# Four more copies of q by DMA, and one logarithm placed behind a copy: an attention kernel fused with a feed-forward network

## The chip, the cores and the metric

The kernel runs on one core of one Trainium2 chip. The metric is the device time in microseconds of one execution of the whole program. Three runs of the kernel before gave 288.22, 288.23 and 288.67 us; the median is 288.23 us.

## The reference

Eight batches of eight heads, 576 tokens, 64 numbers per head. Heads 0 to 3 ("plain") let a token see itself and the 31 tokens before it; heads 4 to 7 ("dilated") let it see every fourth token of the last 128. The result goes through a feed-forward network with a squared ReLU:

```python
scores = scale * np.matmul(q, k.transpose(0, 1, 3, 2))
scores = np.where(masks[None, :, :, :], scores, -1000000000.0)
attn = np.exp(scores - np.max(scores, axis=-1, keepdims=True))
attn = attn / (np.sum(attn, axis=-1, keepdims=True) + 1e-09)
x = np.matmul(attn, v)                       # then (tokens, 512)
h = np.maximum(x @ w_in, 0.0)                # w_in: 512 x 2048
out = h * h @ w_out                          # w_out: 2048 x 512
```

## The kernel before, in words

**The feed-forward network** works on nine tiles of 512 tokens. A tile is 32 *groups* of work. The first sixteen groups multiply by `w_in` (line 989): ScalarE takes each result out of its PSUM bank with a ReLU (line 1002), VectorE squares it (line 1005). The last sixteen groups multiply by `w_out`. From the fifth tile on this second half is done with seven products of half-size blocks, M1 to M7 (line 1152), of which some use sums of blocks that VectorE makes ahead (line 1046, "the sums"). In the fifth and the sixth tile the products run in this order on TensorE: M1, half of M2, M6, the other half of M2, M5, M7, M3, M4. M1, M6 and M5 share one PSUM bank, called X here: after M1 ScalarE copies the bank to SBUF (line 1066), after M6 a second time (line 1068), after M5 a third time (line 1068). M5 cannot start before the second copy has ended, because it overwrites the bank. M2's bank is added up by VectorE (line 1053).

**The attention** is not a stage of its own: its steps are hung between the groups of the network, so that TensorE goes from network to attention and back. All engines take their instructions in the order in which the program records them; nothing is reordered later. A list `steps` holds entries (group, rank, batch, code); it is sorted by group and rank, and after each group the entries that are due are recorded. In the fifth tile (groups 128 to 159, t = 128) the attention of batch 5 is finished, in the sixth tile (t = 160) that of batch 6. A pair of heads is called e (0 and 1 plain, 2 and 3 dilated). The codes that matter:

- `V`, a *visit* (function `quadrants`): TensorE computes scores of some pairs of heads and the products with v and with ones of others, in 64x64 quarters of the array (line 379). The visit at t+15 serves pairs 0 and 2 with products, the one at t+23 serves pairs 1 and 3 and computes the scores of the next batch's pairs 2 and 0.
- `E`: ScalarE's exponential of a score bank (line 745) and VectorE's mask (line 750).
- `L`: the logarithm of a pair's denominators on ScalarE, two instructions, 512 columns (line 712) and 64 columns (line 713). `X`: ScalarE's exponential of minus that logarithm (line 727), then VectorE's two products that write the normalised result to `xT` (lines 730 and 734).
- `K`, `R`, `Q` (function `arrange`): a batch's k, its end pieces and its plain q are put in the layout that the scores read. q and k come from HBM by GpSimd's queue (line 183) and are transposed by DMA from SP's queue into `qx` and `kx` (line 264). `Q` has eight copies for a batch, four of pair 0 and four of pair 1, in each case from one half of the partitions to one half.

The two places that the change touches, before it:

```python
# arrange, lines 342 to 347
if what == "Q" and (b == B - 1 or b == B - 2 and e == 1):
    nc.sync.dma_start(q_both[rows, hs, jj::2, :], qx[b % 2][src, hs, :, :])
elif what == "Q" and b == XB:
    ...
elif what == "Q":
    copy(q_both[rows, hs, jj::2, :], qx[b % 2][src, hs, :, :])

# the steps of a batch from the sixth on (quick), second half of its tile
visit(t + 15, [(b, 3), (b, 1)], [(b, 0), (b, 2)][: 1 + (b >= PAIRED)])
...
expo(3, *[t + 16 + quick] * 2)
norm(0, t + 17 + 2 * quick)          # L0 at t + 19, X0 at t + 20
visit(t + 23, [(b + 1, 2), (b + 1, 0)] if after else [], [(b, 1), (b, 3)])
```

`copy` is VectorE's here, `B` is 8, `quick` holds for batches 5, 6 and 7, and `after` for all but the last batch. So before the change batch 7's eight copies of q and batch 6's four of pair 1 go by DMA from SP's queue (line 343, tile `qT`), and batch 6's four copies of pair 0 are VectorE's (line 347). These four stand at groups 134 and 135, in the first half of the fifth tile. The group t+20 holds the end of M6, and with it the second copy of bank X.

Two rings matter for the order of the work. The visit at t+23 writes the bank `po` that X0's product (line 730) reads, so TensorE waits there for that product. It also needs four `pf` banks, two of which are those of M2 and of M5; TensorE waits for line 1053 and for the third copy before it uses them.

Of the kernel before, what the change touches and what calls it, by code (L numbers as in the profile page):

```python
# [63 lines left out]
def kernel(  # L64
# [11 lines left out]
    B, H, S, D = q.shape  # L76
# [257 lines left out]
    def arrange(b: int, what: str, g: int, jj: int, e=None, copy=nc.vector.tensor_copy):  # L334

        src, rows = sides[jj], sides[g]
        n = H // 2  # L340
        hs = slice(0, n) if e is None else slice(2 * e, 2 * e + 2)
        if what == "Q" and (b == B - 1 or b == B - 2 and e == 1):
            nc.sync.dma_start(q_both[rows, hs, jj::2, :], qx[b % 2][src, hs, :, :])
        elif what == "Q" and b == XB:
            copy(qT[rows, 0:2, jj::2, :], qx[b % 2][src, g:4:2, :, :])
        elif what == "Q":
            copy(q_both[rows, hs, jj::2, :], qx[b % 2][src, hs, :, :])
        elif what == "K":
            nc.vector.tensor_copy(
                k_both[rows, g::2, hs, :].rearrange("p i h (c j m) -> p j (h c) i m", c=2, j=2)[:, jj, :, :, :],  # L350
                kx[b % 2][src, hs, :, :].rearrange("p h c (i m) -> p (h c) i m", m=16)[:, :, g::2, :],
            )
        else:
            ms = (slice(128, M), slice(0, 16))[g]
            copy(
                ends[b % 2][rows, 0, :, :].rearrange("p h (r m) -> p h r m", r=RES)[:, :, jj::2, :], qx[b % 2][src, n:, :, ms]
            )
            copy(
                ends[b % 2][rows, 1, :, :].rearrange("p h (m c j) -> p j h c m", c=2, j=2)[:, jj, :, :, :],
                kx[b % 2][src, n:, :, ms],  # L360
            )
# [337 lines left out]
    def natural_step(b: int, code: str):  # L699
        what, e = code[0], int(code[1])  # L700
        if what == "Z":
            late.pop()()
        elif what in "QKR":
            arrange(b, what, e, int(code[2]), *(int(x) for x in code[3:4]), *[nc.scalar.copy][: len(code) - 4])
        elif what == "V":
            scs, pvs = ([(int(x[0]), int(x[1])) for x in y.split(",") if x] for y in code[2:].split("/"))
# [654 lines left out]
    groups, steps = [], []  # L1361
# [15 lines left out]
    for b in range(NATURAL, B):  # L1377
        t = G * (b - 1)
        early = b == NATURAL
        def visit(at, scs, pvs):  # L1380
            steps.append((at, 2, b, "V0" + "/".join(",".join(f"{x}{y}" for x, y in z) for z in (scs, pvs))))

        def expo(e, *at):
            steps.extend((y, 1, b, f"E{e}{x}") for x, y in enumerate(at))

        def norm(e, at):
            steps.extend([(at, 3, b, f"L{e}"), (at + 1, 0, b, f"X{e}")])

        after = b + 1 < B
        if b < PAIRED:  # L1390
            start = 61 if early else t - 8
            second = t + (7 if early else 5)
            if early:
                visit(start, [], [(XB, 0), (XB, 1)])
                for y, e in enumerate((1, 0)):
                    steps.extend([(start + y, 3, XB, f"L{e}"), (start + y + 1, 0, XB, f"X{e}")])
                visit(second, [(b, 2), (b, 3)], [])
                expo(2, second + 1, second + 2)
                expo(3, second + 4, second + 6)
            else:  # L1400
                expo(2, start + 7, start + 9)
                visit(second, [(b, 0)], [(b, 2)])
                norm(2, second)
                expo(0, second + 3, second + 5)
        if early:
            visit(t + 15, [(b, 0), (b, 1)], [(b, 2), (b, 3)])
            steps.extend((t + 15, 3, b, f"E1{x}") for x in (1, 0))
            norm(3, t + 15)
            expo(0, t + 16, t + 16)
            norm(2, t + 17)  # L1410
            visit(t + 24, [(b + 1, 2)], [(b, 0), (b, 1)])
            norm(0, t + 24)
            norm(1, t + 25)
        else:
            visit(t + 15, [(b, 3), (b, 1)], [(b, 0), (b, 2)][: 1 + (b >= PAIRED)])
            quick = b > FAST
            if not quick:
                steps.extend((t + 15, 3, b, f"E1{x}") for x in range(2))
            else:
                steps.extend((t + 15, 3, b, f"E1{x}e") for x in (1, 0))  # L1420
                steps.extend((t + 16, 1, b, f"E1{x}m") for x in (1, 0))
                steps.append((t + 16, 2, b, "Z0"))
            if b >= PAIRED:
                norm(2, t + 15)
            expo(3, *[t + 16 + quick] * 2)
            norm(0, t + 17 + 2 * quick)
            visit(t + 23, [(b + 1, 2), (b + 1, 0)] if after else [], [(b, 1), (b, 3)])
            if after:
                steps.extend((t + 23, 3, b + 1, f"E0{x}") for x in range(2))
                steps.extend((t + 27 + 2 * x, 1, b + 1, f"E2{x}") for x in range(2))  # L1430
            if quick and after:
                steps.extend([(t + 23, 3, b, "L3"), (t + 24, 3, b, "L1"), (t + 25, 0, b, "X3"), (t + 26, 0, b, "X1")])
            else:
                norm(3, t + 23)
                norm(1, t + 25 - after)
        at = t - (14 if b < PAIRED else 19 if b == PAIRED else 25)
        for x, code in enumerate(("R00", "R01", "R10", "R11")):
            steps.append((start + 3 + x // 2 if early else t - 28 + x // 2 if b > PAIRED else at + x, 1, b, code))
        for x, code in enumerate(("K00", "K01", "K10", "K11", "Q00", "Q01", "Q10", "Q11")):
            if b < PAIRED:  # L1440
                steps.append((start + (2 + x // 2 if x < 4 else 1 + x) if early else t - 6 + x, 1, b, code))
            else:
                if b > PAIRED:
                    steps.append((t - 30 + x // 2 + 2 * (x // 4), 1, b, code + "0"))
                else:
                    steps.append((at + 3 + x % 4 + x // 4, 3, b, code + "0" + "a" * (x // 6)))
                steps.append((t - 8 + x, 1, b, code + "1"))
# [50 lines left out]
```

## Time and profile before

| | |
|---|---|
| median of three runs | 288.23 us (288.22 to 288.67) |
| the profiled execution | 288.85 us |
| its span, first to last instruction | 287.1 us |
| TensorE busy (PE) | 280.1 us, 98% of the span |
| VectorE busy (DVE) | 187.8 us, 65% |
| ScalarE busy (ACT) | 186.4 us, 65% |
| GpSimd busy (POOL) | 123.4 us, 43% |
| mean granted clock of TensorE | 0.998 |

The profile shows one execution. In its rows the first number of a timeline is the start in us from the first instruction, the second the busy time in us; "x16" counts instructions that follow each other in one row; the brackets at the end give the time for which the engine stood idle before, and what released it. PE is TensorE's matmuls, PEld its weight loads, PEldq its queue, SPq SP's queue. Because TensorE is busy nearly all the time, the time of the kernel is moved only by what TensorE waits for; an engine that is idle a third of its time may still be late at one place.

### The profile page before, as it was taken

The page shows a single profiled execution, that of the slowest core. Times are in us where ns is not written, and L with a number is a line of the kernel's source. Part 1 is how long each engine was busy: PE and PEld are TensorE (multiplying, and loading weights), DVE is VectorE, ACT ScalarE, POOL GpSimd, SP SyncE. Part 2 cuts the span into 40 slices and gives each one's busy share as a digit, 9 for nine tenths or more (in the row PEclk, how much of TensorE's full clock was granted, in tenths as well). Part 3 has the DMA queues.
Part 4 walks back from the last instruction along what each step waited for, and adds up shares of the span by engine and source line. Part 5 has one row for each costly group of instructions (what it writes and reads, how often), then busy time and mean ns, then how long its engine had stood idle before and what let it go on. Part 6 is the DMA issues. An engine that isn't in the chain of part 4 may idle for free.

```text
span 287.1 us, 8392 instructions
## 1 busy us (share of the span) xinstructions
PE 280.1 (98%) x3461; PEld 189.4 (66%) x3473; DVE 187.8 (65%) x472; ACT 186.4 (65%) x379; POOL 123.4 (43%) x208
## 2 busy tenths in 40 slices
PE   8999999999999999999999999999999999999995
PEld 7689746958655544554555876588658865885684
DVE  1776315655869766699768978986777627523852
ACT  6888626787848865888756775686568557407620
POOL 8686267672673984857677368700000000000000
PEclk9999999999999999999999999999999999999999
DMA  8999999999999999999999999900320030012004
GB/s 125 194 184 207 206 211 194 187 142 164 177 187 203 173 133 210 156 152 145 128 168 199 134 115 190 182 3 5 116 72 2 2 148 0 0 45 104 0 2 146
DMA packets 87093, 36.67 MB, mean 128 GB/s; under 512 B 56336, under 2 KB 82448, under 8 KB 87056
## 3 DMA queue, kind: packets, MB, share of 16 engines
q0 software_dynamic: 49056, 18.49, 58.1%
q1 hardware_dynamic: 37584, 17.29, 31.3%
q8 instruction: 27, 0.44, 0.6%
q10 hardware_dynamic: 416, 0.36, 0.4%
q14 instruction: 10, 0.08, 0.1%
HBM read 37.50 MB, written 9.44 MB: 164 GB/s over the span
## 4 chain that ended last, share of the span: by engine, by line
PE 67%; DMA 18%; POOL 5%; DVE 4%; issue 3%; ACT 1%; POOLq 0%
PE pf L989 29%; PE pf L1152 20%; PE pf L1192 8%; DMA kb<-in_k_dram 6%; DMA xx<-qb 4%; DMA vbd<-in_v_dram 4%; DMA qb<-in_q_dram 3%; PE po L783 2%; POOL vbd L329 2%; DVE h2T L1005 1%; PE po L379 1%; POOL qb L183 1%; PE pa L813 1%; POOL vbd L321 1%; PE pf L379 1%
## 5 line engine op out<-in xcount | busy, mean ns | idle before, releaser
L989 PE MATMUL pf<-xT,w_in 128*128 128x512 bf16 (+1 forms) x704 | 127.9, 341 | 0.0
L989 PEld LDWEIGHTS <-w_in 128*128 128x128 bf16 x704 | 78.1, 114 | 45.3 <-issue 0.3
L1002 ACT ACTIVATE h2T<-pf 128x512 bf16<-128x512 f32 x143 | 83.8, 600 | 34.0 <-PE pf L989 33.7
L1005 DVE TENSOR_TENSOR h2T<-h2T 128x512 bf16<-128x512 bf16 (+1 forms) x109 | 53.7, 508 | 34.8 <-ACT h2T L1002 33.3
L1192 PE MATMUL pf<-w_out_sb,h2T 128*128 128x512 bf16 x244 | 56.0, 379 | 1.1 <-issue 0.6
L329 POOL DMA_DIRECT2D vbd<-in_v_dram x80 | 43.4, 553 | 23.0 <-DMA qb<-in_q_dram 9.4
L1192 PEld LDWEIGHTS <-h2T 128*128 128x128 bf16 x256 | 24.3, 98 | 27.9
L1152 PEld LDWEIGHTS <-h2T 128*128 128x128 bf16 x320 | 30.8, 98 | 4.2
L1152 PE MATMUL pf<-w_out_sb,h2T 128*128 128x256 bf16 x160 | 19.3, 273 | 0.0
L1053 DVE TENSOR_TENSOR whole<-pf,whole 128x512 f32<-128x512 f32 (+2 forms) x19 | 12.0, 633 | 11.1 <-PE pf L1152 10.3
L1152 PE MATMUL pf<-kb,h2T 128*128 128x256 bf16 x160 | 19.1, 273 | 0.0
L1152 PE MATMUL pf<-qb,qb 128*128 128x256 bf16 x160 | 18.6, 272 | 0.5 <-ACT whole L1068 0.5
L1152 PEld LDWEIGHTS <-qb 128*128 128x128 bf16 x160 | 15.7, 98 | 2.4 <-issue 0.6
L183 POOL DMA_DIRECT2D qb<-in_q_dram x19 | 13.7, 720 | 7.4 <-DMA xx<-qb 5.0
L727 ACT ACTIVATE rec<-rec 128x576 f32<-128x576 f32 x24 | 16.3, 691 | 0.5
L205 POOL DMA_DIRECT2D vbd<-in_v_dram x16 | 10.9, 685 | 13.0 <-DMA kb<-in_k_dram 9.4
L1198 ACT COPY osb<-pf 128x512 f32<-128x512 f32 x14 | 8.2, 585 | 12.4 <-PE pf L1192 12.4
L745 ACT ACTIVATE pt<-pa 128x384 bf16<-128x384 f32 (+1 forms) x26 | 12.0, 497 | 6.3 <-DVE xT L734 5.6
L183 POOL DMA_DIRECT2D kb<-in_k_dram x19 | 13.1, 692 | 6.0 <-DMA w_in<-in_moe_w_in_dram 2.1
L321 POOL DMA_DIRECT2D vbd<-in_v_dram x20 | 12.0, 612 | 4.9 <-DMA vbd<-in_v_dram 3.9
L315 POOL DMA_DIRECT2D vd<-in_v_dram x20 | 12.1, 615 | 1.4 <-issue 0.7
L730 DVE TENSOR_TENSOR xT<-pf,rec 128x512 bf16<-128x512 f32 x11 | 7.6, 689 | 7.0 <-ACT rec L727 7.0
(178 smaller groups left out, 392.2 us busy)
## 6 DMA issues: line engine op xcount, KB each, us to landing
out_dram<-whole SPq DMA_DIRECT2D x6, 512.0 KB, 3.2
qb<-in_q_dram POOLq DMA_DIRECT2D x7, 320.0 KB, 6.9
kb<-in_k_dram POOLq DMA_DIRECT2D x7, 320.0 KB, 10.6
vd<-in_v_dram POOLq DMA_DIRECT2D x34, 64.0 KB, 5.5
w_out_sb<-in_moe_w_out_dram POOLq DMA_DIRECT2D x4, 512.0 KB, 13.7
out_dram<-osb SPq DMA_DIRECT2D x16, 128.0 KB, 6.0
out_dram<-osb SPq DMA_DIRECT2D x8, 256.0 KB, 5.9
qb<-in_q_dram POOLq DMA_DIRECT2D x6, 256.0 KB, 8.0
```

The lines of the kernel that those rows point to most:

```text
L183: nc.gpsimd.dma_start(t[p0 : p0 + n, part, h0:h1, :], src[b, h0:h1, t0 : t0 + RES * n, :].rearrange("h (p r) d -> p h (r d)", r=RES),)
L315: nc.gpsimd.dma_start(vds[b][rows, e, :, :], v[b, H // 2 + 2 * e + (hl ^ crossed(b, e + NE // 2)), 0:512, :].rearrange("(m p r) d -> p m ( ...
L321: nc.gpsimd.dma_start(v_rows[b % 2][rows, NE // 2 :, i, :], v[b, H // 2 + hl : H - turn_[0] : 2 + turn_[1], 64 * i : 64 * i + 64, :].rearr ...
L329: nc.gpsimd.dma_start(v_rows[b % 2][p0 + 16 * r : p0 + 16 * r + 16, e, :, :], v[b, 2 * e + hl, :, :].rearrange("(i m r) d -> r m i d", r=R ...
L727: nc.scalar.activation(rec[:, :], rec[:, :], ACT.Exp, scale=-1.0)
L745: nc.scalar.activation(pt, sp[b, e][g][:, 0:n], ACT.Exp, scale=SCALE)
L989: nc.tensor.matmul(to, w_in_sb[piece][:, kt, c0 : c0 + 509 : 4], rhs, start=(kt == kts[0] and x == 0), stop=(kt == kts[-1] and x == per - ...
L1002: nc.scalar.activation(hv, acc[u][:, :].rearrange("p (x n) -> p x n", x=per), ACT.Relu)
L1005: nc.vector.tensor_tensor(out=hv, in0=hv, in1=hv, op=ALU.mult)
L1053: nc.vector.tensor_tensor(out=to, in0=one, in1=two_, op=ALU.add)
L1152: nc.tensor.matmul(cur[bank][:, i, y0:y1], lhs(f, i), rhs(f)[:, y0:y1], start=f == 0 and (piece or name in fresh and i == 0), stop=f == NF ...
L1192: nc.tensor.matmul(cur[m][:, c0:c1], h2[:, f, P * m : P * m + P], w_out_sb[:, f, c0:c1], start=(f == 0), stop=(f == NF - 1),)
```

## The change

Batch 6's four copies of pair 0's plain q are issued as DMAs from SP's queue in place of VectorE's copies, at the same place in the program. And for batches 5 and 6 the two logarithms L0 move from group t+19 to group t+20, where they are recorded behind the second copy of bank X and directly ahead of X0.

```diff
-        if what == "Q" and (b == B - 1 or b == B - 2 and e == 1):
+        if what == "Q" and b >= B - 2:
             nc.sync.dma_start(q_both[rows, hs, jj::2, :], qx[b % 2][src, hs, :, :])
...
             expo(3, *[t + 16 + quick] * 2)
-            norm(0, t + 17 + 2 * quick)
+            if quick and after:
+                steps.extend([(t + 20, -1, b, "L0"), (t + 20, 0, b, "X0")])
+            else:
+                norm(0, t + 17 + 2 * quick)
```

In the built program ScalarE's order around the second copy was, in both tiles: two exponentials (line 745), the logarithms (712, 713), the copy (1068), the exponential of X0 (727). It becomes: two exponentials, the copy, the logarithms, the exponential of X0. VectorE loses four instructions of line 347, SP's queue gains four of line 343 behind three stores of line 953 and ahead of batch 7's transposes. TensorE's matmuls keep their order. The waits that stand in TensorE's queue as instructions of their own are 61 before and after, but at the fifth tile's visit at t+23 one of them, which stood behind the first scores, now stands ahead of them, because it waits for the DMAs of q. The two banks that the visit takes over from M2 and M5 change their roles: the products with v of pair 3 take M5's, and the products with ones M2's.

## The prediction

> **What bounds the kernel now.** I read the page's busy times first, then the busy time by stage for the second halves of the two tiles that the change touches.
>
> ```profile
> PE 280.1 (98%) x3461; PEld 189.4 (66%) x3473; DVE 187.8 (65%) x472; ACT 186.4 (65%) x379; POOL 123.4 (43%) x208
> 159.93:174.27 14.34, 13.87 (x221) 12.16 (x215) 12.58 (x33) 9.58 (x22) 9.14 (x17) 1.00 1.31 127
> 189.38:202.91 13.53, 13.53 (x221) 12.04 (x216) 10.92 (x30) 9.58 (x22) 0.00 (x0) 1.00 0.02 4
> ```
>
> TensorE is busy for 98% of the span, so a saving elsewhere counts only where TensorE waits for it. The two windows run from M1's first matmul to the next tile's first and hold the same work, 221 matmul rows each. The fifth tile's takes 14.34 us, the sixth's 13.53 us. If the change made the fifth as short as the sixth, it would save 0.81 us. That is the ceiling of the gain, 0.28% of the profiled execution's 288.85 us. A measurement of this kernel tells about 0.2%, or 0.58 us, from no change.
>
> Next, the timeline of the fifth tile shows where the 0.81 us lies.
>
> ```profile
> 162.56 1.91 PE L1152 MATMUL pf<-qb,qb 128*128 128x256 bf16 x16
> 163.81 0.87 ACT L745 ACTIVATE pt<-pa 128x384 bf16<-128x384 f32 x2 [1.33 <-DVE xT L734]
> 164.56 0.60 ACT L712 ACTIVATE rec<-pd 128x512 f32<-128x512 f32 x1
> 165.04 0.24 ACT L713 ACTIVATE rec<-pa 128x64 f32<-128x64 f32 x1
> 165.15 0.62 ACT L1068 COPY whole<-pf 128x512 f32<-128x512 f32 x1
> 165.61 0.73 ACT L727 ACTIVATE rec<-rec 128x576 f32<-128x576 f32 x1
> 165.81 1.91 PE L1152 MATMUL pf<-qb,qb 128*128 128x256 bf16 x16 [0.47 <-ACT whole L1068]
> 166.64 0.69 DVE L730 TENSOR_TENSOR xT<-po,rec 128x512 bf16<-128x512 f32 x1
> 167.70 0.38 PE L379 MATMUL pf<-qT,kbd 64*64 64x96 bf16 x17
> ```
>
> And the sixth tile, which has the same steps:
>
> ```profile
> 192.01 1.91 PE L1152 MATMUL pf<-qb,qb 128*128 128x256 bf16 x16
> 193.96 0.59 ACT L1068 COPY whole<-pf 128x512 f32<-128x512 f32 x1 [0.57 <-PE pf L1152]
> 194.44 0.69 ACT L727 ACTIVATE rec<-rec 128x576 f32<-128x576 f32 x1
> 194.63 1.91 PE L1152 MATMUL pf<-qb,qb 128*128 128x256 bf16 x16
> 195.16 0.69 DVE L730 TENSOR_TENSOR xT<-po,rec 128x512 bf16<-128x512 f32 x1 [0.34 <-ACT rec L727]
> 195.90 0.68 DVE L1053 TENSOR_TENSOR whole<-pf,whole 128x512 f32<-128x512 f32 x1
> 196.48 0.39 PE L379 MATMUL pf<-qT,kbd 64*64 64x96 bf16 x17
> ...
> 197.21 0.28 PE L379 MATMUL pf<-pt,ones 64*64 64x64 bf16 x2
> ```
>
> I count each tile from the start of M6 (162.56 and 192.01). M5 starts at 3.25 in the fifth and at 2.62 in the sixth: 0.63 us is lost, because the second copy comes behind the logarithms at 2.59 instead of 1.95, where in the sixth tile it starts as soon as M6 has ended. The visit's scores start at 5.14 and 4.47, which is 0.67, so another 0.04 is lost by there. The remaining 0.14 (0.81 less 0.67) is lost inside the visit.
>
> The last reading is of TensorE's queue. A wait that does not fit on a matmul stands in it as an instruction of its own:
>
> ```profile
> L379 PEldq EVENT_SEMAPHORE  x3: 51/51/51, 167.4 to 167.6; - x3
> L379 PEldq EVENT_SEMAPHORE  x1: 51/51/51, 167.9 to 167.9; - x1
> L379 PEldq EVENT_SEMAPHORE  x4: 51/51/51, 195.9 to 196.2; - x4
> ```
>
> Each group's first row starts as X0's product (line 730) ends: 166.64 + 0.69 = 167.33 before 167.4, and 195.16 + 0.69 = 195.85 before 195.9. So at the visit the queue is held by this product, in the sixth tile too, and the waits behind it pass one by one, four starts in about 0.35 us. In the sixth tile they end at about 196.3, and the scores start at 196.48 because the array needs that long after M5. There the product has only 0.18 us in hand.
>
> **The copies of q.**
>
> ```profile
> 154.17 0.68 DVE L347 COPY qT<-xx 64x576 bf16<-64x576 bf16 x2
> 158.36 0.63 DVE L347 COPY qT<-xx 64x576 bf16<-64x576 bf16 x2
> 160.89 0.68 ACT L727 ACTIVATE rec<-rec 128x576 f32<-128x576 f32 x1
> 161.89 0.59 ACT L1066 COPY whole<-pf 128x512 f32<-128x512 f32 x1 [0.31 <-PE pf L1152]
> 162.96 0.68 DVE L730 TENSOR_TENSOR xT<-pf,rec 128x512 bf16<-128x512 f32 x1
> ```
>
> VectorE loses 0.68 + 0.63 = 1.31 us, and the timeline shows it without a pause of note from there to X2's product at 162.96. That product moves to 161.65; it cannot pass 161.57, where its exponential ends (160.89 + 0.68). ScalarE's two exponentials, which wait for that step, move from 163.81 to 162.50, behind the first copy (161.89 + 0.59 = 162.48), and end at about 163.4. M6 ends at 164.51 (162.56 + 1.95). By then the logarithms would have ended as well, had they stayed in front: 163.4 + 0.6 + 0.2. So the copies' removal alone frees M5, and the move of L0 buys nothing more there.
>
> What comes in their place:
>
> ```profile
> qT<-xx SPq DMA_DIRECT2D x8, 72.0 KB, 3.2
> L343 SPq DMA_DIRECT2D qT<-xx x12: 592/629/1244, 176.6 to 207.3; - x12
> 151.33 0.19 DVE L355 COPY kbd<-xx 64x128 bf16<-64x128 bf16 x1 [0.66 <-DMA xx<-qb]
> 151.30:162.60 11.30, 11.30 (x162) 7.29 (x161) 10.89 (x25) 8.44 (x16) 6.78 (x11) 1.00 1.26 183
> 162.61 2.21 SPq L264 DMA_TRANSPOSE xx<-kb  x1
> 168.60 3.40 SPq L264 DMA_TRANSPOSE xx<-qb  x1
> DMA to landing us min/median/max: 4.4/6.5/11.7
> 179.75 0.19 DVE L355 COPY kbd<-xx 64x128 bf16<-64x128 bf16 x1
> ```
>
> Batch 6's q lands at 151.3, where VectorE's wait for it ends. Four issues of 0.63 us keep SP's queue until about 153.8; batch 7's transposes stand behind them, but start at 162.61 anyway. The last DMA lands some 3.2 us later, at 157, and q is first read at 167.7 (166.6 even if four landings of 3.2 us came one after the other): nothing waits for it. The DMA engines are crowded there. Four times 72 KB at the window's 183 GB/s is 1.6 us, my estimate of what it can put off batch 7's loads and so its transposes (0 to 4 us as ends: nothing, or one landing of 3.2 us and an issue). The last transpose lands at 168.60 + 6.5 = 175.1, with 1.6 more at 176.7, and VectorE reads it at 179.75. I cost it at nothing; the cover is 3 us.
>
> **The logarithms behind the copy.** From the copy's start, the next ScalarE instruction starts 0.46 to 0.48 us later (165.15 to 165.61, 193.96 to 194.44), the second logarithm 0.48 after the first (164.56 to 165.04), and X0's exponential needs the second one's end, 0.24 and a handover of 0.04 (the copy's end at 165.77, M5 at 165.81). So L0 stands for 0.48 + 0.28 = 0.76 us ahead of X0 wherever the copy does not wait for ScalarE. From below it cannot be less than the two starts, 0.48 + 0.11; from above it is the full durations with the copy's, 0.95 (below).
>
> *Sixth tile.* The copy still starts at 193.96, since it waits for TensorE. X0's product moves from 195.16 to 195.92 and ends at 196.61. The held wait passes at 196.65, the fourth at 197.0, and the scores start at about 197.06 instead of 196.48: **0.58 us lost** (0.76 less the 0.18 in hand). If only the first wait counted and the others ran beside the array, the visit would start 0.23 late; these are the ends, and I take 0.58, because the fifth tile's rows show the waits passing in turn. Behind the product VectorE has line 1053, whose bank the visit's products with ones need now; it moves along, from 195.90 to 196.66, and ends at 197.34, ahead of those products (197.21 and 0.58 more). Behind the copy ScalarE has, besides L0 and X0, only the third copy, which waits for M5 and finds ScalarE free at 195.9.
>
> *Fifth tile.* With VectorE and ScalarE in time it now runs as the sixth does, counted from M6: copy 1.95, X0's exponential 1.95 + 0.48 + 0.76 = 3.19, product 0.72 later (194.44 to 195.16) at 3.91, its end at 4.60, scores at 5.05. Before they stood at 5.14, so M5's 0.63 is given back at the visit but for **0.09 us gained**. The wait at 167.9, behind the first scores, now stands ahead of them and is in the 5.05; I take the 0.14 lost inside the visit as its cost and **gained** (ends 0 and 0.18).
>
> Sum: 0.58 − 0.09 − 0.14 = +0.35 us. The profiled execution's 288.85 us becomes 289.20. What lies around the span (1.75 us) doesn't move, and the median of the runs, 0.62 us under that execution, goes from 288.23 to 288.58.
>
> The Trainium skill ("Perfetto Trace Analysis", Identifying Dependency Chains) says that an instruction which waits for several engines may have EventSemaphore instructions put ahead of it. By that rule, the rows agree, with four of them ahead of the scores; the page names no price, and without one the sixth tile would lose 0.23 and the sum would be 0.00.
>
> **The rivals.** *The waits behind the product run beside the array.* Then both visits start 0.23 later than they could: the fifth gains 0.81 − 0.23 = 0.58, the sixth loses 0.23, net −0.35 us, 287.88. For it: in the sixth tile before, waits passed while M5 still ran. Against it: in the fifth they passed at 167.4 to 167.6 and the scores came at 167.70. Chance 0.18.
>
> *Behind the copy the logarithms don't overlap: slower.* If each instruction starts only when the one before has ended, X0's exponential comes 0.59 + 0.60 + 0.24 = 1.43 after the copy instead of 1.24. The sixth tile loses 0.77, the fifth gains 0.04 with its 0.14, net +0.73 us, 288.96. It decides from 0.12 us of missing overlap (two tiles, 0.35 + 0.24). For it: no row quoted here has a logarithm right behind such a copy. Against it: the starts 0.48 apart above. The Trainium skill ("ScalarE: Activation LUTs", Rules for kernel authors) budgets about 0.3 us per ACTIVATE and 0.83 ns an element; an estimate by it is 1.08 us for 512 and 64 elements, and the sum would be about +1.0. The rows' durations of 0.60 and 0.24 speak against it. Chance 0.16.
>
> *Batch 7's transposes come too late: slower.* If the crowding puts them off by more than 4.6 us, VectorE stops at 179.75 with the tile's squares behind it; at 6 us that is up to 1.4 us, 289.6. Chance 0.05.
>
> *The gain without the loss*, X0's product in time in both tiles: −0.81 us, 287.42. It needs ScalarE to have the logarithms done before M6's end, which the new order forbids. Chance 0.06.
>
> **How the numbers follow.** The forecast has 0.55; its own range is 288.4 to 288.8. Faster by over 0.2% (under 287.65) is the last rival, 0.06. Slower by over 0.2% (over 288.81) is the two slower rivals, 0.21, and the forecast's upper end, 0.06: 0.27. Within 0.2% is the rest, 0.67. The range 287.85 to 289.0 takes in the forecast, the first rival and the second.
>
> **What would show it.** In the changed kernel's profile: no line 347 in the fifth tile, and line 343 at about 151 to 154; the exponentials at about 162.5; no idle TensorE ahead of M5; the logarithms behind the copy in both tiles; the product of line 730 some 0.75 us later after M6 in the sixth tile, and the waits in TensorE's queue right behind its end, with the scores 5.05 us after M6's start in both tiles; windows of about 14.1 us in both. The prediction is wrong if the sixth window stays at 13.5, or if a wait for a DMA holds the scores or VectorE.

## The result, and the profile after

The changed kernel takes 289.85 us (median of 8 runs, 289.55 to 290.63), the kernel before 288.40 us in the same session (8 runs, 288.22 to 289.67): a ratio of 1.0047, 95% interval 1.0028 to 1.0065. That is 1.45 us slower. Ratios, here and below, are worked out from the runs that fall in no slow state, and not from the two medians, so the two can differ. The forecast was 288.58 us, with 289.0 as its upper end.

The profiled execution of the changed kernel took 289.78 us. Its page shows four VectorE instructions fewer, TensorE's busy time raised by 0.4 us and the span by 0.9 us:

```profile
span 288.0 us, 8394 instructions
PE 280.5 (97%) x3461; PEld 189.5 (66%) x3473; DVE 186.8 (65%) x468; ACT 186.8 (65%) x379; POOL 123.0 (43%) x208
```

The busy time by stage (length of the window in us, then busy us and instructions of PE, PEld, DVE, ACT, POOL, then the granted clock, the DMA share and GB/s) gives the two windows of the changed kernel, fifth tile first:

```profile
160.26:174.42 14.16, 13.91 (x219) 12.28 (x215) 11.08 (x30) 9.78 (x22) 10.47 (x20) 1.00 1.16 130
189.53:203.64 14.11, 13.87 (x219) 12.21 (x215) 10.92 (x30) 9.79 (x22) 0.00 (x0) 1.00 0.01 4
```

Both are 14.1 us long, as forecast. In the timeline of the fifth tile after the change, each step is where the prediction had put it:

```profile
162.79 0.87 ACT L745 ACTIVATE pt<-pa 128x384 bf16<-128x384 f32 x2
162.89 1.91 PE L1152 MATMUL pf<-qb,qb 128*128 128x256 bf16 x16
164.84 0.59 ACT L1068 COPY whole<-pf 128x512 f32<-128x512 f32 x1 [1.17 <-PE pf L1152]
165.32 0.60 ACT L712 ACTIVATE rec<-pd 128x512 f32<-128x512 f32 x1
165.51 1.91 PE L1152 MATMUL pf<-qb,qb 128*128 128x256 bf16 x16
166.07 0.68 ACT L727 ACTIVATE rec<-rec 128x576 f32<-128x576 f32 x1
166.78 0.69 DVE L730 TENSOR_TENSOR xT<-po,rec 128x512 bf16<-128x512 f32 x1 [1.08 <-ACT rec L727]
167.99 0.36 PE L379 MATMUL pf<-qT,kbd 64*64 64x96 bf16 x17
```

M6 starts at 162.89 and M5 2.62 later, with no idle time. ScalarE stands idle 1.17 us until M6 lets go of the bank, and only then makes the logarithms. The bracket at line 730 shows where they went: VectorE waits 1.08 us for X0's exponential. The sixth tile shows the same, counted from M6 at 192.16:

```profile
192.16 1.91 PE L1152 MATMUL pf<-qb,qb 128*128 128x256 bf16 x16
194.10 0.59 ACT L1068 COPY whole<-pf 128x512 f32<-128x512 f32 x1 [1.17 <-PE pf L1152]
195.34 0.68 ACT L727 ACTIVATE rec<-rec 128x576 f32<-128x576 f32 x1
196.05 0.69 DVE L730 TENSOR_TENSOR xT<-po,rec 128x512 bf16<-128x512 f32 x1 [1.08 <-ACT rec L727]
197.25 0.36 PE L379 MATMUL pf<-qT,kbd 64*64 64x96 bf16 x17
```

Last, the queue of TensorE and its waits in the changed kernel:

```profile
L379 PEldq EVENT_SEMAPHORE  x4: 51/51/51, 167.5 to 167.9; - x4
L379 PEldq EVENT_SEMAPHORE  x4: 51/51/51, 196.8 to 197.1; - x4
PE po L379 <- DVE xT L734: 0.4, 2, 0.2
```

In both tiles the four waits pass as X0's product ends (166.78 + 0.69 = 167.47 and 196.05 + 0.69 = 196.74). TensorE is idle for only 0.2 us each time by the waits view, but the scores start 5.10 and 5.09 us after M6.

So the two profiled executions differ by −0.18 us in the fifth window and +0.58 us in the sixth, +0.40 us together, where +0.35 was forecast. The runs differ by 1.45 us. The rest is the question.

### The profile page after: what moved, and what is told of

Same layout as the page of the kernel before. It is cut to its first block, busy times and chain, and to the rows that moved or that the text cites. A ratio compares the mean times of both kernels' runs of the same rounds, so it can differ in the third digit from the quotient of the medians.

```text
span 288.0 us, 8394 instructions
## 1 busy us (share of the span) xinstructions
PE 280.5 (97%) x3461; PEld 189.5 (66%) x3473; DVE 186.8 (65%) x468; ACT 186.8 (65%) x379; POOL 123.0 (43%) x208
## 4 chain that ended last, share of the span: by engine, by line
PE 91%; ACT 2%; DMA 2%; DVE 1%; issue 1%; POOL 1%; POOLq 0%
PE pf L989 42%; PE pf L1152 20%; PE pf L1192 19%; DMA kb<-in_k_dram 2%; PE po L379 2%; PE pf L379 2%; PE pa L379 2%; ACT h2T L1002 1%; PE pa L813 1%; PE pd L379 1%; PE pf L865 0%; ACT rec L727 0%; POOL qb L183 0%; PE pa L574 0%; DVE h2T L1005 0%
## 5 line engine op out<-in xcount | busy, mean ns | idle before, releaser
L730 DVE TENSOR_TENSOR xT<-po,rec 128x512 bf16<-128x512 f32 x13 | 9.0, 689 | 5.4 <-ACT rec L727 5.3
```

## The experiments

The theories that the expectations name are these. *Theory 1*: the change acts in the two tiles alone, and what is left lies in how an execution starts. *Theory 2*: q's DMAs cost time outside the two tiles too. *Theory 3*, formed after the first four: the 0.8 us that the fifth tile loses in the first profile of before depends on when batch 6's transposes land, it is missing in other executions, and so the change costs some 0.6 us in each tile. Its rival: the loss is there in each execution, and the rest lies elsewhere.

In these sessions single runs spread further (287.7 to 296.4 us over all kernels), so the intervals of the ratios are wide. I read the experiments by the windows of their profiles and give medians beside them. The kernel before was run again beside each set: its median is 289.74 us beside a to d (35 runs, 287.73 to 295.17), 288.67 beside e to h (35 runs) and 288.70 beside i to k (18 runs). The intervals of all eight ratios from a to h take in 1, so the times alone tell none of these kernels, the changed one among them, from the kernel before; the argument rests on their profiles. Only the shortest runs of the first set hint at the same: 287.73 for before, 287.80 for b, 289.20 for c, 289.39 for d. In the table the windows are in us, and the last two columns count from the start of M6.

| kernel | fifth window | sixth window | scores after M6, fifth | M5 after M6, fifth |
|---|---|---|---|---|
| before, first profile | 14.34 | 13.53 | 5.14 | 3.25 |
| a: before again | 14.07 | 13.52 | 4.98 | 3.10 |
| e: before, third profile | 13.54 | 13.53 | 4.47 | 2.62 |
| b: copies of q alone | 14.89 | 13.53 | 5.41 | 3.40 |
| h: copies of q alone, again | 13.57 | 13.53 | 4.47 | 2.62 |
| c: logarithms alone | 14.02 | 14.14 | 4.97 | 2.62 |
| f: logarithms, sixth tile alone | 13.55 | 14.12 | 4.47 | 2.62 |
| g: logarithms, fifth tile alone | 14.03 | 13.53 | 4.97 | 2.62 |
| after, first profile | 14.16 | 14.11 | 5.10 | 2.62 |
| d: after again | 14.15 | 14.11 | 5.13 | 2.62 |
| i: before, transposes late | 17.66 | 13.52 | 5.50 | 3.65 |
| j: after, transposes late | 15.36 | 14.12 | 5.41 | 2.79 |
| k: copies of q alone, transposes late | 14.93 | 13.53 | 5.41 | 3.40 |

**a: the kernel before, unchanged.**

> The kernel before, unchanged, as a measure of how far one program's runs and profiles lie apart. Theory 1 (the change acts in the two tiles alone, and the rest of the measured 1.45 us belongs to how a build starts): its span lies within 0.6 us of 286.5 to 287.1 us, the fifth tile's window is 14.3 us, the sixth's 13.5 us, and the stretch ahead of 20 us differs between two profiles of this same program by some tenths of a us. Theory 2 (the DMAs of q cost time outside the two tiles): the stretch ahead of the fifth tile is the same to 0.1 us in each profile of this program.

289.09 us (12 runs; ratio 1.0008, 0.9965 to 1.0052). The fifth window is 14.07, not 14.34 as in the first profile: one program gives two lengths. It also starts 0.87 us later, at 160.80 us instead of 159.93; so the stretch ahead of it differs between two profiles of one program, against Theory 2's 0.1 us.

```profile
160.80:174.87 14.07, 13.76 (x220) 12.11 (x215) 12.24 (x34) 9.47 (x22) 8.69 (x16) 1.00 1.15 124
```

**b: the copies of q alone.**

```diff
-        if what == "Q" and (b == B - 1 or b == B - 2 and e == 1):
+        if what == "Q" and b >= B - 2:
```

> Only batch 6's four copies of q go by DMA; L0 stays where it was. Theory 1: ScalarE is in time for the second copy, X0's product too, so the fifth tile's window falls from 14.34 to about 13.5 us (0.8 us faster) and the sixth's stays at 13.5; the whole is faster by up to 0.8 us, less what the start of this build adds. Theory 2 (the DMAs cost elsewhere): the fifth window falls as well, but the whole is slower than before by 0.2 to 0.7 us, and the loss lies outside the two windows.

288.72 us (ratio 0.9984, 0.9950 to 1.0019). Both theories had the fifth window fall to about 13.5 us; it is longer than before the change, 14.89 us. The timeline of VectorE shows why:

```profile
150.12 0.64 DVE L349 COPY kbd<-xx 64x320 bf16<-64x320 bf16 x2 [1.65 <-DMA xx<-kb]
153.75 0.19 DVE L355 COPY kbd<-xx 64x128 bf16<-64x128 bf16 x1 [1.61 <-DMA xx<-qb]
```

VectorE stands idle for 3.26 us until batch 6's transposes land, ahead of the place of the four copies. In the first profile of before the same two lines wait too, the second for 0.66 us (quoted in the prediction), the first for 0.76 us:

```profile
148.84 0.62 DVE L349 COPY kbd<-xx 64x320 bf16<-64x320 bf16 x2 [0.76 <-DMA xx<-kb]
```

**c: the logarithms alone, in both tiles.**

```diff
-            norm(0, t + 17 + 2 * quick)
+            if quick and after:
+                steps.extend([(t + 20, -1, b, "L0"), (t + 20, 0, b, "X0")])
+            else:
+                norm(0, t + 17 + 2 * quick)
```

> Only L0 moves behind the second copy of bank X; the copies of q stay VectorE's. Theory 1: M5 starts 0.6 us earlier in the fifth tile, but X0's product is VectorE's at the same time as before (166.6 us), so the fifth window stays at 14.3 us; the sixth window grows by 0.6 us to 14.2; the whole is slower by 0.6 us. Theory 2 agrees on the windows, and has nothing outside them, as no DMA is added: 0.6 us slower, where the changed kernel is 1.45 slower.

289.65 us (ratio 1.0014, 0.9986 to 1.0042). Its two windows:

```profile
160.39:174.41 14.02, 13.78 (x221) 12.16 (x215) 11.65 (x32) 9.81 (x22) 10.49 (x20) 1.00 1.09 124
189.52:203.66 14.14, 13.88 (x219) 12.21 (x215) 10.91 (x30) 9.78 (x22) 0.00 (x0) 1.00 0.01 4
```

The moved logarithms alone make both windows long: in this execution no wait for a DMA stands at line 349 or 355, so nothing else lengthens the fifth.

**d: the changed kernel again.**

> The changed kernel once more. Theory 1: the two windows are 14.1 us each (0.2 us shorter and 0.6 longer), the whole is slower than before by 0.4 us plus what the start adds; if that start is a matter of the single run, this time's ratio lies near 1.0015, if it belongs to the build, near 1.0047 again. Theory 2: near 1.0047 again, with more than 0.3 us between the start and the fifth tile.

289.83 us (ratio 1.0019, 0.9988 to 1.0050). Its windows are those of the first profile after, within 0.01 us, although line 349 waited 0.79 us for a DMA in this execution and not in the first. By its time, this repeat could not be told from the kernel before.

**e: the kernel before, a third profile.**

> The kernel before, unchanged, once more, for its profile and its runs. Theory 3 (formed from the first four runs: the 0.8 us that the fifth tile lost in the first profile is a matter of when batch 6's transposes land in an execution, and is missing in most): a profile whose time is near 288.2 has windows of about 13.5 us in both tiles, and line 349 or 355 waits little or not at all for its DMA; the change then costs 0.6 us in each tile, 1.2 in all. Rival (the fifth tile's loss is there in each execution, and the rest of the 1.45 us lies elsewhere): the window of the fifth tile is 14.0 to 14.4 us at any time of the execution.

288.63 us (ratio 0.9984, 0.9952 to 1.0017). This profile decides for Theory 3. No wait for a DMA stands at line 349 or 355, and the fifth window, the first row here, is as short as the sixth:

```profile
160.41:173.95 13.54, 13.54 (x221) 12.06 (x215) 11.41 (x32) 9.58 (x22) 9.96 (x19) 1.00 1.13 129
189.05:202.58 13.53, 13.53 (x221) 12.04 (x215) 10.93 (x30) 9.58 (x22) 0.00 (x0) 1.00 0.02 4
```

TensorE is busy for every microsecond of it. In the timeline of ScalarE and TensorE there:

```profile
163.14 0.87 ACT L745 ACTIVATE pt<-pa 128x384 bf16<-128x384 f32 x2 [0.19 <-DVE xT L734]
163.90 0.60 ACT L712 ACTIVATE rec<-pd 128x512 f32<-128x512 f32 x1
164.99 0.58 ACT L1068 COPY whole<-pf 128x512 f32<-128x512 f32 x1 [0.37 <-PE pf L1152]
165.66 1.91 PE L1152 MATMUL pf<-qb,qb 128*128 128x256 bf16 x16
167.51 0.39 PE L379 MATMUL pf<-qT,kbd 64*64 64x96 bf16 x17
```

The exponentials and both logarithms (the second, of 0.24 us, starts at 164.37) are done before M6 ends, the copy waits for TensorE (0.37 us) and not for ScalarE, and M5 follows without a gap. This execution has nothing for the change to gain.

What differs between executions is when batch 6's transposes come. The first of the four in the first profile of before, and then in e:

```profile
139.30 1.26 SPq L264 DMA_TRANSPOSE xx<-kb  x1
137.77 2.11 SPq L264 DMA_TRANSPOSE xx<-kb  x1
```

The first is issued 20.6 us ahead of M1 in the first profile of before, 20.2 in a and 20.2 in b: these three lose time. It is issued 22.6 ahead in e, 22.5 in h and 21.7 in f: these three lose nothing. The issue is not the whole of it: a and b start alike, and VectorE waits 1.24 us for the transposes in a and 3.26 in b. So three of the six profiled executions that had the logarithms in their old place lost 0.5 to 1.4 us in the fifth tile.

**f and g: the logarithms in one tile alone.** The diff is that of c with `if b == 6:` (f) and `if b == 5:` (g) as its condition.

> L0 behind the copy in the sixth tile alone; the copies of q stay VectorE's. Both theories: sixth window 14.1 us, 0.6 us slower than before (ratio 1.002), fifth window as before, 13.5 to 14.3.

> L0 behind the copy in the fifth tile alone; the copies of q stay VectorE's. Theory 3: the fifth window is 14.0 us as in the first run with L0 alone, which is 0.5 us more than in most executions of the kernel before, so the whole is 0.5 us slower (ratio 1.0017). Rival: 0 to 0.3 us faster than before, as the fifth window falls from 14.3 to 14.0.

f: 289.19 us (ratio 1.0003, 0.9975 to 1.0031); g: 289.45 us (1.0011, 0.9984 to 1.0037). The sixth window of f and the fifth of g:

```profile
188.69:202.81 14.12, 13.88 (x222) 12.25 (x215) 10.92 (x30) 9.78 (x22) 0.00 (x0) 1.00 0.02 4
159.73:173.76 14.03, 13.79 (x222) 12.17 (x215) 11.94 (x32) 9.82 (x22) 10.75 (x20) 1.00 1.10 125
```

Each move costs in its own tile and leaves the other's window as it was: 0.59 us in the sixth, 0.49 us in the fifth against e. With the copies of q (the changed kernel) the fifth is 0.13 us longer still, 14.16, and its scores come 0.13 us later: the wait for q's DMAs stands ahead of the scores there, and the four waits in TensorE's queue start some 0.12 us apart.

**h: the copies of q alone, again.** The diff is that of b.

> Only the four copies of q by DMA, once more, on another chip or at another time. Theory 3: no difference in most executions (ratio 0.998 to 1.001), since VectorE is in time without it; where batch 6's transposes land late, the fifth window is long with it too. Rival: faster by 0.8 us (ratio 0.997), because the fifth tile's loss is there always and this takes it away.

288.66 us (ratio 1.0007, 0.9970 to 1.0044); fifth window 13.57 us. In an execution in which the transposes come early, the copies of q bring nothing to the tile, since nothing is lost there.

**i, j and k: the transposes put later**, in the kernel before (i), after (j) and with the copies of q alone (k). Batch 6's transposes are issued eight groups later:

```diff
-    CROSS = {b: G * (b - 1) - 44 for b in range(6, B)}
+    CROSS = {b: G * (b - 1) - (36 if b == 6 else 44) for b in range(6, B)}
```

> The kernel before, with batch 6's four transposes put eight groups later in SP's queue (behind two of the three stores that followed them), so that they land late in each execution. Theory 3 (the landing of these transposes decides the fifth tile's window, by way of VectorE's copies that wait for it): lines 349 and 355 wait for DMA by 2 to 6 us in all, and the fifth window grows to 14.3 to 17 us, with the idle time ahead of M5 or earlier; the sixth stays at 13.5. Rival (the fifth window's 0.8 us in the first profile had another cause): the fifth window stays near 13.5.

> The changed kernel with the same late transposes. Theory 3: here the copies' removal has something to give: the fifth window is shorter than that of the late kernel before by 0.2 to 1.2 us, the sixth is 14.1, so the whole lies between 0.4 us slower and 0.6 faster than the late kernel before. Rival: 0.6 us longer in both windows, 1.2 slower.

> Only the four copies of q by DMA, with the same late transposes. Theory 3: the shortest of the three late ones, by 0.3 to 1.3 us in the fifth window against the late kernel before, and 13.5 in the sixth. Rival: the same as the late kernel before.

292.42 us (i, 4 runs; ratio 1.0118, 1.0036 to 1.0200), 291.79 us (j, 9 runs; 1.0123, 1.0089 to 1.0157) and 290.52 us (k, 10 runs; 1.0061, 1.0023 to 1.0099). The fifth windows of i, j and k:

```profile
161.53:179.19 17.66, 15.83 (x221) 12.57 (x215) 15.08 (x39) 9.59 (x22) 11.04 (x21) 0.90 1.03 129
160.35:175.71 15.36, 14.55 (x220) 11.89 (x216) 13.47 (x36) 9.69 (x22) 8.39 (x16) 1.00 1.21 136
160.30:175.23 14.93, 14.17 (x220) 12.03 (x216) 12.98 (x35) 9.55 (x22) 8.06 (x16) 1.00 1.22 142
```

Line 349 waits 4.08 us for its DMA in i, 3.94 in j and 3.24 in k. Later transposes do lengthen the fifth window, as Theory 3 needs, and k is the shortest of the three; the sizes were missed. i lies above the forecast 14.3 to 17 us, and j and k are shorter than i by 2.30 and 2.73 us, where 0.2 to 1.2 and 0.3 to 1.3 were forecast. Not all of that is the worth of the four copies: line 349 waited least in k, and nearly all of the 2.73 us lies between the starts of M1 and M6 (5.73 us in i, 3.06 in k), where in i TensorE waits for VectorE's squares and its clock falls (last section).

What the logarithms do in a late execution is seen from M6 on, in j and then in k:

```profile
163.90 1.91 PE L1152 MATMUL pf<-qb,qb 128*128 128x256 bf16 x16
169.31 0.36 PE L379 MATMUL pf<-qT,kbd 64*64 64x96 bf16 x17
163.36 1.91 PE L1152 MATMUL pf<-qb,qb 128*128 128x256 bf16 x16
168.77 0.36 PE L379 MATMUL pf<-qT,kbd 64*64 64x96 bf16 x17
```

The scores come 5.41 us after M6 in both. With the logarithms behind the copy M5 starts 0.61 us earlier, and the visit gives that back; the 0.43 us by which j's fifth window is longer lie ahead of M6 (3.55 us after M1 in j, 3.06 in k), where TensorE waits twice for VectorE's squares in j and the moved logarithms do not yet stand. So in these profiles the move costs its 0.5 us in the fifth tile when the transposes come early, and nothing there when they come this late. In the sixth tile it costs 0.59 us here too (14.12 to 13.53).

**The end of the program.** Theory 2 also holds, for a small part. I compared from the last sum of VectorE (line 1053) to the end of the span. Its start and, by the waits of SP's queue, what SP waited for after it (us in total, times, longest): before, then after the change. Lines 1493 and 1496 are the same line; the change adds three lines above it.

```profile
283.53 0.29 DVE L1053 TENSOR_TENSOR whole<-pf,whole 128x128 f32<-128x128 f32 x1 [0.15 <-PE pf L1152]
SPq L1493 <- DMA out_dram<-whole: 1.5, 3, 0.6
```

```profile
284.26 0.29 DVE L1053 TENSOR_TENSOR whole<-pf,whole 128x128 f32<-128x128 f32 x1 [0.15 <-PE pf L1152]
SPq L1496 <- DMA out_dram<-whole: 1.6, 1, 1.6
```

From there to the end it is 287.1 − 283.53 = 3.57 us before and 288.0 − 284.26 = 3.74 us after. In the seven profiles without the four new DMAs it is 3.49 to 3.58 (three waits, the longest 0.6 us), in the six with them 3.72 to 3.77 (one wait of 1.6 or 1.7 us): 0.20 us by the means. SP's list of waits at the program's end meets the last output in another place. That the waits which now stand behind it make the difference was not tried by itself.

The account closes so, against an undisturbed execution of before (e): 14.16 − 13.54 = 0.62 us in the fifth tile, 14.11 − 13.53 = 0.58 in the sixth, 0.20 at the end: 1.40 us of the 1.45 by which the medians differ. Between the two windows (15.1 us) and from the sixth's end to the last sum (80.62 us) before, e and after agree to 0.01 us. The stretch ahead of the fifth window belongs to the execution, as Theory 1 has it: it is 159.93, 160.80 and 160.41 us in the three profiles of before, and 160.26 and 160.34 in the two of after. No experiment ended measurably below the kernel before; the copies of q alone, which the windows pointed to, ran twice and could not be told from it.

## Why the prediction was wrong, step by step

- **The step that failed is the ceiling.** The prediction read "the fifth tile's takes 14.34 us, the sixth's 13.53 us" as the kernel's state, costed the fifth tile at −0.09 − 0.14 = −0.23 us from there, and carried the sum over to the median by taking off 0.62 us. But much of what the profiled execution had above the median can be this very loss, so it was counted as a gain and then taken off again. In e the fifth window of before is 13.54 us, so the term is +0.62 us and not −0.23. The signs of it were there: two waits of VectorE for a transpose (0.76 and 0.66 us, the second quoted for another purpose), and an execution 0.62 us above its own median with no place found for it. The 0.14 us inside the visit was part of the same: from the scores to the window's end it is 6.57 us in the first profile of before, 6.43 after the change, but 6.44 in e and 6.45 in f too, so it was not the price of a wait that stands behind the first scores.
- **The sixth tile** was right: 0.58 us forecast, 0.58 measured, and the scores 5.05 us after M6 forecast, 5.09 measured. c and f, with the logarithms alone, lose the same there.
- **The fifth tile after the change** was right: a window of about 14.1 us forecast, 14.16 measured, the scores at 5.10 after M6, M5 at 2.62 without idle time. Only what it was compared with was not.
- **The logarithms' price** was right: X0's exponential comes 1.24 us after the copy's start (194.10 to 195.34), 0.48 before the change, hence 0.76 us. The rival without overlap needed 1.43. The Trainium skill ("ScalarE: Activation LUTs", Rules for kernel authors) gave an estimate of 1.08 us for the two, by a rule stated for a bias that is a pointer operand; the trace's 0.76 decides.
- **The waits in TensorE's queue** pass one behind the other, as forecast: four of them right behind the product in both tiles, where the rival had them run beside the array and the windows at 13.8.
- **"The copies' removal alone frees M5"** was not run at the lateness of the first profile. d comes near it (0.79 us at line 349): there ScalarE stands idle for 1.17 us between the exponentials and the copy after M6, room for the two logarithms (0.60 + 0.24 us), so the reading fits. Where the transposes land later it is not so: in b line 355 is released at 153.75 us instead of 151.33, and without the four copies M5 still comes 3.40 us after M6. In e and h there is nothing to free. The prediction took the landing of the transposes as fixed.
- **The DMAs of q at nothing** was right inside the two tiles, but for the wait ahead of the scores, which the 5.05 had counted in; 0.20 us at the end of the program was missed: "what lies around the span doesn't move" was said, and the stretch from the last sum to the end was not looked at.
- **Batch 7's transposes** did not come late: no profile of the changed kernel shows a wait for them.
- **Still open:** what puts the transposes of batch 6 1 to 3 us earlier or later from one execution to the next, and what share of the timed runs of before loses time to it. Three of six profiles did. That the eight runs behind the median of 288.40 mostly did not is inferred from the sum of 1.40 us, not shown run by run.

## What to carry to other kernels

Before a gain is read from a stage of one profile, ask whether that stage's loss belongs to the program or to that execution: an idle time ahead of it that a DMA ends, and a profiled time above the median, both say that it may be the execution. A second and a third profile of the unchanged kernel can settle it. Price an edit against the execution without the loss: there all that it adds is paid, and what it saves is nothing.

## What the runs showed of the hardware

In i, TensorE's clock fell. The waits of TensorE in the fifth window of i, and its busy time by stage there (columns as above; the clock is the third number from the end):

```profile
PE pf L1152 <- DVE h2T L1005: 1.8, 3, 1.4
162.50:164.50 2.00, 0.47 (x3) 0.11 (x2) 1.94 (x6) 0.68 (x1) 0.67 (x2) 1.00 1.69 182
164.50:165.95 1.45, 1.15 (x8) 0.62 (x9) 1.42 (x5) 0.00 (x0) 0.65 (x3) 1.00 0.51 32
165.95:169.35 3.40, 3.40 (x18) 2.44 (x17) 3.33 (x9) 1.92 (x5) 1.97 (x4) 0.50 0.92 135
169.35:170.90 1.55, 1.55 (x16) 1.36 (x14) 1.52 (x5) 0.81 (x4) 1.55 (x4) 1.00 0.98 112
```

Three waits for VectorE's squares, 1.8 us together and none over 1.4, left TensorE busy for 0.47 + 1.15 = 1.62 us of 3.45. Then the granted clock was 0.50 for 3.40 us, and 1.00 again. At half speed those 3.40 us do 1.70 us of work, by my estimate, so the stall cost its 1.8 us and 1.7 more, 3.5 of the 4.1 us by which the window is longer. The Trainium skill ("TensorE: Matmul & The Clock Gate", Part 1: The HAM clock gate) describes half the clock after an idle window of about 3.4 us, and full clock again after about 3.4 us of sustained work. The depth and the length agree with this trace; but here no idle piece was over 1.41 us, and the clock fell after a stretch of 3.45 us that was 47% busy. In j, two waits of 0.2 us each in the same place left the clock at 1.00. One execution shows the drop; what share of idle time it takes was not tried.
